# Reordering the first stage of a fused attention and snake-MLP kernel: g product before the rsqrts, one chunk squared on GpSimd, weights loaded later

## Chip, cores, metric

One NeuronCore of a Trainium2 chip, one launch. The metric is the device time in microseconds (us) of one execution, median of several. "Span" is the profiled time from the first to the last instruction, some 2 us less than the device time. A DMA "lands" when all its data has arrived. The "software queue" carries the DMAs that GpSimd issues, the "hardware queue" those of SyncE and ScalarE.

## The reference

```python
q_n, k_n = rmsnorm(q, g_q), rmsnorm(k, g_k)     # q, k, v: 8 batches, 12 heads, 448 tokens, 64
attn = softmax(q_n @ k_n.T / 8)
x = (attn @ v)                                   # as 3584 tokens x 768
h = x @ w_in                                     # 768 x 2048
g = h + sin(alpha * h) ** 2 / (alpha + 1e-9)     # "snake"
out = g @ w_out                                  # 2048 x 768
```

## The kernel before

The kernel runs in stages. In the first, q and k of batch 0 are normalised in three "chunks" of two head pairs, transposed, and made into scores, exponentials and attention values. Then comes the first product of batch 0 (`hps`, 192 matmuls), with the snake step beside it. From there each stage does the attention of the next batch, with the second product of the batch before (`ops`, 896 matmuls in all) cut into fillers between. The program's order is the order on each engine. `S_(n)` is one score tile with n blank matmuls ahead, `A_()` one attention product, `step_of(c, …)` the norm steps of a chunk (0 and 1: squares on GpSimd, 2: the g product folded in, 3 and 4: sums on VectorE, 5: rsqrt and scaling, 6: transposes by DMA and the load of chunk c + 3). NC is 3, so `NC` and `NC + 1` are the fourth and fifth chunk. A "bank" is a piece of PSUM, the memory that TensorE writes; `g_sb` holds the results of the snake step, `osb` the copy of a finished output tile that frees its bank. The first product goes in "pairs" of two snake tiles, counted from 0.

```python
def load_w_in():                              # f32 in memory, bf16 in SBUF, issued by GpSimd
    for hi in range(2):
        nc.gpsimd.dma_start(out=w_in_sb[hi * 64:hi * 64 + 64], in_=rows[hi])
def load_w_out(half):                         # 768 columns in two halves of 384
    nc.gpsimd.dma_start(out=w_out_sb[:, :, cols], in_=src[:, :, cols])
# ... first stage
c0.square(1), c0.square(0)
c0.reduce(1), c0.reduce(0)
c0.rsqrt(slice(1, 2)), c0.rsqrt(slice(0, 1))
keep_busy(BUSY[0], blank)                     # 20 blank matmuls
spread_g()                                    # g_q * g_k to all partitions: matmul, then a ScalarE copy
keep_busy(BUSY[1], blank)                     # 8
c0.fold_g()
# ... v loads, gate on the third chunk
load_w_in()
# ...
S_(), S_(), S_()
c1.rsqrt()
S_(3)
c2.square(0), c2.square(1)                    # on ScalarE
# ...
load_w_out(0)
begin_norm(NC); step_of(NC, 0, 1, 2)()
# ... scores, attention products, fourth and fifth chunk
v_parts[2](), v_parts[3]()
load_w_out(1)                                 # before the first product
A_(), A_()
step_of(NC + 1, 5, 6)()
first_product(0, beside_h(0))
```

"Gate" is a one-column GpSimd copy of a chunk's tile: it holds GpSimd, and so the DMA issues behind it, until that chunk has landed.

Of the kernel before, what the change touches and what calls it, by code (L numbers as in the profile page):

```python
# [32 lines left out]
def kernel(  # L33
# [37 lines left out]
    HALF = D_MODEL // 2  # L71
    BUSY = (20, 8)

# [85 lines left out]

    w_in_sb = wpool.tile([P, KT, D_FF], BF16)  # L160
    w_out_sb = wpool.tile([P, MT, D_MODEL], BF16)
# [19 lines left out]

    def load_w_in():

        rows = moe_w_in.rearrange("(hi pr d) f -> hi d pr f", hi=2, d=D)
        for hi in range(2):
            nc.gpsimd.dma_start(out=w_in_sb[hi * 64:hi * 64 + 64], in_=rows[hi])

# [15 lines left out]
    def norm_tasks(ci):  # L203
# [5 lines left out]
        st.ms = npool.tile([P, 2, 2 * NJ], F32, tag="ms", name="ms")  # L209
        st.inv, st.inv_ps, st.scaled = {}, None, 0  # L210
        st.sq, st.n = {}, None

        def square(w):
            if early:
                rows = g_sb[:, 4 * ci + 2 * w:4 * ci + 2 * w + 2, :].rearrange("p m s -> p (m s)")
                st.sq[w] = rows.bitcast(F32).rearrange("p (a d) -> p a d", d=D)
                nc.scalar.activation(st.sq[w], qk[ci][:, w], ACT.Square)
            else:
                st.sq[w] = npool.tile([P, 2 * NJ, D], F32, tag="sq", name="sq")
                nc.gpsimd.tensor_mul(st.sq[w], qk[ci][:, w], qk[ci][:, w])  # L220
# [7 lines left out]
        def rsqrt(ws=slice(0, 2)):  # L228
            ln = npool.tile([P, 2, 2 * NJ], F32, tag="inv", name="inv")
            if early and st.inv_ps is None:  # L230
                st.inv_ps = bank_pair("inv")
            inv = st.inv_ps[:, :, :2 * NJ] if early else ln
            for w in range(2)[ws]:
                st.inv[w] = inv[:, w, :]
            nc.scalar.activation(ln[:, ws], st.ms[:, ws, :], ACT.Ln, scale=1.0 / D, bias=eps)
            nc.scalar.activation(inv[:, ws], ln[:, ws], ACT.Exp, scale=-0.5)  # L236

        def scale(w):
            eng = nc.vector if early else nc.gpsimd
            if st.n is None:  # L240
                st.n = npool.tile([P, 2, NJ, 2, D], BF16, tag="qkn", name="qkn")
            n, x = st.n[:, w], qk[ci][:, w].rearrange("p (hi j) d -> p hi j d", hi=2)
            inv = st.inv[w].rearrange("p (hi j) -> p hi j", hi=2)
            for hi in range(2):
                eng.tensor_mul(n[:, :, hi, :], x[:, hi], inv[:, hi].unsqueeze(2).to_broadcast([P, NJ, D]))  # L245
            st.scaled += 1
            if early and st.scaled == 2:
                give_back(st.inv_ps, passes() + 3.0)

# [47 lines left out]

    def attend(pi):


        b, hp = pi // NP, pi % NP
        av = bank_pair("av")
        for j in range(NJ):
            for part in range(2):
                for hi in range(2):
                    r = key_rows(pi, hi)
                    o = slice((hi + part) % 2 * 64, (hi + part) % 2 * 64 + 64)
                    nc.tensor.matmul(av[o, part, :S], ones[r, :] if part else vb[b][r, hp, j, :],  # L308
                                     expT[pi // 2, j][r, pi % 2, :], start=(j == 0), stop=(j == NJ - 1))
        rec = rpool.tile([P, S], F32, tag="rec", name="rec")  # L310
        nc.scalar.activation(rec, av[:, 1, :S], ACT.Ln)  # L311
        nc.scalar.activation(rec, rec, ACT.Exp, scale=-1.0)  # L312
        if hp == 0:
            xT[b] = xpool.tile([P, KT, S], BF16, tag="xT", name="xT")
        for hi in range(2):
            r, o = slice(hi * 64, hi * 64 + 64), slice(64 - hi * 64, 128 - hi * 64)
            nc.vector.tensor_mul(xT[b][r, hp, :], av[r, 0, :S], rec[o, :])  # L317
        give_back(av, passes(1.32, 1.06) + 1.4)

# [17 lines left out]
    def first_product(b, beside):  # L337
# [4 lines left out]
        def mm(ps, m, kts):  # L342
            for kt in kts:
                nc.tensor.matmul(ps[:, m % 2, :S], w_in_sb[:, kt, m * P:(m + 1) * P], x[:, kt, :],  # L344
                                 start=(kt == 0), stop=(kt == KT - 1))
# [72 lines left out]
    c0.reduce(1), c0.reduce(0)  # L418
    c0.rsqrt(slice(1, 2)), c0.rsqrt(slice(0, 1))
    keep_busy(BUSY[0], blank)  # L420
    spread_g()
    keep_busy(BUSY[1], blank)
    c0.fold_g()
# [7 lines left out]
    nc.gpsimd.tensor_copy(gate, qk[2][:, 1, 0, 0:1])  # L431
    load_w_in()
    norm[2] = c2 = norm_tasks(2)
    c0.scale(1), c0.scale(0)
    c0.pe_transpose((0, 1), (1,), act=True)
# [11 lines left out]
    def beside_h(b):  # L447

        ci = NC * b + 5
        if ci >= NC * B:  # L450
            return {}
        return {0: [lambda: begin_norm(ci)], 1: [step_of(ci, 0)], 3: [step_of(ci, 1)], 4: [step_of(ci, 3)],
                5: [step_of(ci, 2)], MT // 2: [step_of(ci, 4)]}

    def stage(b):

        tiles = deque((b * NC + c, j) for c in range(NC) for j in range(NJ))
        pairs = deque(b * NP + p for p in range(NP))
        return (lambda warm=0: scores(*tiles.popleft(), warm)), (lambda: attend(pairs.popleft()))

    S_, A_ = stage(0)
    S_(), S_(), S_()
    c1.rsqrt()
    S_(3)
    c2.square(0), c2.square(1)
    c2.fold_g()
    c1.scale(0), c1.scale(1)
    load_qk(NC)
    S_(2), S_(1), S_()
    c1.pe_transpose((0, 1))  # L470
# [5 lines left out]
    load_qk(NC + 2)  # L476
    load_w_out(0)
    begin_norm(NC)
    step_of(NC, 0, 1, 2)()
    A_(), S_(1), S_(1), S_(1)  # L480
    c2.pe_transpose((0, 1))
    v_parts = load_v(1)
    v_parts[0](), v_parts[1]()
    begin_norm(NC + 1)
    step_of(NC + 1, 0, 1, 2)()
    S_(), S_(), S_()
    step_of(NC, 3, 4)()
    A_(), S_(1), A_(), S_(1)
    step_of(NC, 5, 6)()
    S_(1), A_(), S_(1)  # L490
    step_of(NC + 1, 3, 4)()
    S_()
    v_parts[2](), v_parts[3]()
    load_w_out(1)
    A_(), A_()
    step_of(NC + 1, 5, 6)()
    first_product(0, beside_h(0))


# [3 lines left out]
    for b in range(1, B):  # L503
# [9 lines left out]
        if b + 1 < B:  # L513
            at[2] += [lambda: begin_norm(c3), step_of(c3, 0, 1, 2)]
            at[10] += [lambda: begin_norm(c4), step_of(c4, 0, 1)]
            for slot, task in ((9, step_of(c3, 3)), (10, step_of(c3, 4)), (12, step_of(c3, 5)), (12, step_of(c4, 2)),
                               (13, step_of(c4, 3)), (15, step_of(c4, 4)), (17, step_of(c3, 6)), (18, step_of(c4, 5)),
                               (23, step_of(c4, 6))):
                at[slot].append(task)
            for n, part in enumerate(load_v(b + 1)):  # L520
                at[19 + n].append(part)
# [47 lines left out]
```

## Time and profile before

| | before |
|---|---|
| time, us | 441.9 (441.68 to 442.11, 3 runs) |
| span of the profiled run, us | 440.3 |
| TensorE busy | 425.9 us, 97% |
| first product of batch 0 begins | 44.41 |
| second half of w_out issued, landed | 45.62, 70.4 (24.8 us later) |
| second half of w_out needed (49th matmul of the output product) | 74.42 |

The views of this kernel are quoted in the prediction. In the timeline of TensorE stand start, duration, engine, line, operation, count, and in brackets the idle time before it and its releaser.

### The profile page before, as it was taken

What the parts mean: (1) busy time and instruction counts of PE and PEld (TensorE: products, weight loads), DVE (VectorE), ACT (ScalarE), POOL (GpSimd) and SP (SyncE); (2) the same over time, 40 slices, a digit from 0 to 9 for tenths busy, and PEclk for the clock granted to TensorE, in tenths of its full rate; (3) what the DMA queues carried; (4) which work ended last, traced back from release to release, by engine and by line L of the source; (5) the groups of instructions that cost most, each with busy time, mean ns of one, the idle gap of its engine ahead of it and who ended that gap; (6) DMA issues with size and microseconds to landing.
All of it is one profiled execution on the core that took longest, in us unless ns stands there. A gap on an engine that the chain in (4) does not pass through costs nothing.

```text
span 440.3 us, 9454 instructions
## 1 busy us (share of the span) xinstructions
PE 425.9 (97%) x3811; PEld 220.4 (50%) x3811; DVE 228.1 (52%) x331; ACT 340.1 (77%) x531; POOL 278.0 (63%) x262
## 2 busy tenths in 40 slices
PE   7788999899999999999999999999999999999996
PEld 3234544455555554555555555555555555555563
DVE  3576573456544564464645464545645474246611
ACT  4879888878888788887878788887878788788600
POOL 3867978937698287947599196965599285002300
PEclk9679999999999999999999999999999999999999
DMA  7899999592066803596064902598054900420022
GB/s 251 179 237 251 196 220 226 140 227 78 2 197 180 189 2 76 151 221 120 2 198 146 222 2 51 151 207 159 2 162 116 124 0 18 97 56 1 1 71 73
DMA packets 69296, 55.09 MB, mean 125 GB/s; under 512 B 41460, under 2 KB 65796, under 8 KB 69252
## 3 DMA queue, kind: packets, MB, share of 16 engines
q1 hardware_dynamic: 56690, 40.97, 37.2%
q0 software_dynamic: 11616, 11.81, 17.2%
q10 hardware_dynamic: 946, 1.70, 1.0%
q8 instruction: 30, 0.49, 0.5%
q14 instruction: 14, 0.11, 0.1%
HBM read 45.62 MB, written 11.01 MB: 129 GB/s over the span
## 4 chain that ended last, share of the span: by engine, by line
PE 85%; ACT 4%; POOL 3%; issue 2%; DVE 2%; DMA 2%; SPq 0%; POOLq 0%; DVEq 0%
PE hps L344 33%; PE ops L389 32%; PE av L308 12%; PE sc L292 8%; ACT expT L295 3%; POOL sq L220 2%; DMA g_rows<-in_g_q_dram 1%; POOL qk L223 1%; DMA out_dram<-osb 1%; DVE qkn L245 1%; POOL qkn L245 1%; DVE ms L226 0%; ACT rec L311 0%; PE tp L267 0%; DVE g_sb L331 0%
## 5 line engine op out<-in xcount | busy, mean ns | idle before, releaser
L295 ACT ACTIVATE expT<-sc 128x896 bf16<-128x896 f32 x168 | 145.0, 913 | 33.5 <-PE sc L292 32.2
L389 PE MATMUL ops<-w_out_sb,g_sb 128*128 128x384 bf16 x896 | 156.8, 327 | 0.8 <-DVE osb L395 0.7
L344 PE MATMUL hps<-xT,w_in_sb 128*128 128x448 bf16 x768 | 146.7, 353 | 0.0
L326 POOL TENSOR_TENSOR s<-s 128x448 f32<-128x448 f32 x64 | 59.2, 930 | 101.8 <-ACT s L323 91.0
L389 PEld LDWEIGHTS <-g_sb 128*128 128x128 bf16 x896 | 83.1, 98 | 70.9 <-issue 19.5
L331 DVE SCALAR_TENSOR_TENSOR g_sb<-s,inv_alpha_sb,hps 128x448 bf16<-128x448 f32 x128 | 80.7, 678 | 63.1 <-POOL s L326 63.1
L344 PEld LDWEIGHTS <-w_in_sb 128*128 128x128 bf16 x768 | 74.5, 98 | 71.5 <-issue 2.9
L323 ACT ACTIVATE s<-hps,alpha_sb 128x448 f32<-128x448 f32 x128 | 74.5, 627 | 28.0 <-PE hps L344 26.2
L245 POOL TENSOR_TENSOR qkn<-qk,inv 128x448 bf16<-128x448 f32 x84 | 76.1, 937 | 21.8 <-ACT inv L236 21.3
L317 DVE TENSOR_TENSOR xT<-av,rec 64x448 bf16<-64x448 f32 x96 | 59.7, 622 | 52.9 <-ACT rec L312 33.8
L220 POOL TENSOR_TENSOR sq<-qk 128x896 f32<-128x896 f32 x42 | 69.9, 1678 | 6.1 <-DVE ms L226 4.7
L308 PE MATMUL av<-expT,vb 64*64 64x448 bf16 x672 | 70.4, 353 | 1.2 <-ACT expT L295 1.1
L308 PE MATMUL av<-expT,ones 64*64 64x448 bf16 x672 | 70.4, 353 | 0.0
L226 DVE TENSOR_REDUCE ms<-sq 128x14 f32<-128x896 f32 x42 | 45.3, 1083 | 27.5 <-POOL sq L220 27.2
L292 PE MATMUL sc<-qkT 64*64 64x448 bf16 x672 | 52.1, 369 | 2.7 <-DVE qkT L274 1.1
L395 DVE COPY osb<-ops 128x768 f32<-128x768 f32 (+1 forms) x35 | 27.9, 797 | 50.0 <-PE ops L389 44.1
L223 POOL TENSOR_TENSOR qk<-qk,gg 128x896 f32<-128x896 f32 x24 | 50.1, 2088 | 4.9 <-ACT gg L171 3.3
L308 PEld LDWEIGHTS <-vb 64*64 64x64 bf16 x672 | 37.8, 108 | 15.4 <-issue 3.3
L308 PEld LDWEIGHTS <-ones 64*64 64x64 bf16 x672 | 37.3, 108 | 10.8
L328 ACT ACTIVATE s<-s 128x448 f32<-128x448 f32 x64 | 36.9, 577 | 2.9
L292 PEld LDWEIGHTS <-qkT 64*64 64x64 bf16 x672 | 15.1, 106 | 30.6 <-issue 25.8
L311 ACT ACTIVATE rec<-av 128x448 f32<-128x448 f32 x48 | 26.2, 546 | 3.6 <-PE av L308 3.1
(43 smaller groups left out, 138.9 us busy)
## 6 DMA issues: line engine op xcount, KB each, us to landing
qk<-in_q_dram SPq DMA_DIRECT2D x24, 448.0 KB, 4.9
qk<-in_k_dram SPq DMA_DIRECT2D x22, 448.0 KB, 5.4
out_dram<-osb SPq DMA_DIRECT2D x39, 192.0 KB, 2.9
vb<-in_v_dram POOLq DMA_DIRECT2D x32, 168.0 KB, 6.6
w_in_sb<-in_moe_w_in_dram POOLq DMA_DIRECT2D x2, 1536.0 KB, 20.0
w_out_sb<-in_moe_w_out_dram POOLq DMA_DIRECT2D x2, 1536.0 KB, 27.5
out_dram<-osb SPq DMA_DIRECT2D x26, 96.0 KB, 5.8
qk<-in_k_dram ACTq DMA_DIRECT2D x2, 448.0 KB, 6.0
```

Source lines behind the costliest of these rows:

```text
L220: nc.gpsimd.tensor_mul(st.sq[w], qk[ci][:, w], qk[ci][:, w])
L223: eng.tensor_mul(qk[ci][:, 0], qk[ci][:, 0], gg.to_broadcast([P, 2 * NJ, D]))
L245: eng.tensor_mul(n[:, :, hi, :], x[:, hi], inv[:, hi].unsqueeze(2).to_broadcast([P, NJ, D]))
L292: nc.tensor.matmul(sc[key_rows(pp, hi), pp, :S], qkt[r, 1, j * REST:(j + 1) * REST], qkt[r, 0, :], start=True, stop=True)
L295: nc.scalar.activation(expT[c, j], sc[:, :, :S], ACT.Exp, scale=SCALE)
L308: nc.tensor.matmul(av[o, part, :S], ones[r, :] if part else vb[b][r, hp, j, :], expT[pi // 2, j][r, pi % 2, :], start=(j == 0), stop=(j == ...
L317: nc.vector.tensor_mul(xT[b][r, hp, :], av[r, 0, :S], rec[o, :])
L323: nc.scalar.activation(s1, hps, ACT.Sin, scale=alpha_sb[:, m, :])
L326: nc.gpsimd.tensor_mul(s2, s1, s1)
L331: nc.vector.scalar_tensor_tensor(g_sb[:, m, (b % 2) * S:(b % 2 + 1) * S], s2, inv_alpha_sb[:, m, :], hps, op0=ALU.mult, op1=ALU.add)
L344: nc.tensor.matmul(ps[:, m % 2, :S], w_in_sb[:, kt, m * P:(m + 1) * P], x[:, kt, :], start=(kt == 0), stop=(kt == KT - 1))
L389: nc.tensor.matmul(st["ps"][:, k, :HALF], lhsT, w_out_sb[:, m, half * HALF:(half + 1) * HALF], start=(m == 0), stop=(m == MT - 1))
```

## The change

The intent is an earlier first product: the g product no longer stands behind two rsqrts on ScalarE; ScalarE gives two squares to GpSimd; more blank matmuls and a new order of scores keep the TensorE clock up; the fifth chunk, which GpSimd needs, gets the DMA before half of w_in and all of w_out. Core of the diff, cuts marked:

```diff
-    BUSY = (20, 8)
+    BUSY = (11, 15)
-    w_in_sb = wpool.tile([P, KT, D_FF], BF16)
+    w_in_sb = [wpool.tile([P, KT, D_FF // 2], BF16, name=f"w_in_{half}") for half in range(2)]
...                                            # load_w_in(half), matmuls and rsqrt banks accordingly
-            if early:
+            if ci < 2:                         # third chunk: squares on GpSimd
...
-    c0.rsqrt(slice(1, 2)), c0.rsqrt(slice(0, 1))
     keep_busy(BUSY[0], blank)
     spread_g()
+    c0.rsqrt(slice(1, 2)), c0.rsqrt(slice(0, 1))
...
-    load_w_in()
+    load_w_in(0)
+    c2.square(0), c2.square(1)
+    c2.fold_g()
...                                            # scores with 0 0 | 3 | 3 2 2 1 fillers
     load_qk(NC + 2)
-    load_w_out(0)
     begin_norm(NC)
     step_of(NC, 0, 1, 2)()
+    nc.gpsimd.tensor_copy(gate, qk[NC + 1][:, 1, 0, 0:1])
+    load_w_in(1)
+    begin_norm(NC + 1)
+    step_of(NC + 1, 0, 1, 2)()
...
+    load_w_out(0)                              # behind the fourth chunk's scaling
+    v_parts = load_v(1)
+    v_parts[0](), v_parts[1]()
...                                            # the last two attention products side by side: A_(2)
-    v_parts[2](), v_parts[3]()
-    load_w_out(1)
-    A_(), A_()
-    first_product(0, beside_h(0))
+    for i, task in ((2, v_parts[2]), (4, v_parts[3]), (5, lambda: load_w_out(1))):
+        beside.setdefault(i, []).append(task)  # inside the first product
+    first_product(0, beside)
...                                            # later stages: sums of a chunk one slot later
-            ((9, step_of(c3, 3)), (10, step_of(c3, 4)), ..., (13, step_of(c4, 3)), ...
+            ((10, step_of(c3, 3)), (11, step_of(c3, 4)), ..., (14, step_of(c4, 3)), ...
```

More of the change, by code (lines that the diff above doesn't have):

```diff
@@ L180, in spread_alpha, with load_w_in @@
         nc.vector.reciprocal(inv_alpha_sb, alpha_sb)
-    def load_w_in():
+    def load_w_in(half):
         rows = moe_w_in.rearrange("(hi pr d) f -> hi d pr f", hi=2, d=D)
+        cols = slice(half * D_FF // 2, (half + 1) * D_FF // 2)
         for hi in range(2):
-            nc.gpsimd.dma_start(out=w_in_sb[hi * 64:hi * 64 + 64], in_=rows[hi])
+            nc.gpsimd.dma_start(out=w_in_sb[half][hi * 64:hi * 64 + 64], in_=rows[hi, :, :, cols])
     def load_w_out(half):
@@ L209, in norm_tasks @@
         st.ms = npool.tile([P, 2, 2 * NJ], F32, tag="ms", name="ms")
-        st.inv, st.inv_ps, st.scaled = {}, None, 0
+        st.inv, st.inv_ps, st.scaled = {}, [], 0
         st.sq, st.n = {}, None
         def square(w):
-            if early:
+            if ci < 2:
                 rows = g_sb[:, 4 * ci + 2 * w:4 * ci + 2 * w + 2, :].rearrange("p m s -> p (m s)")
@@ L229, in rsqrt @@
             ln = npool.tile([P, 2, 2 * NJ], F32, tag="inv", name="inv")
-            if early and st.inv_ps is None:
-                st.inv_ps = bank_pair("inv")
-            inv = st.inv_ps[:, :, :2 * NJ] if early else ln
+            inv = bank_pair("inv") if early else ln
+            if early:
+                st.inv_ps.append((inv, passes(0.0, 0.55) + 2.4))
             for w in range(2)[ws]:
-                st.inv[w] = inv[:, w, :]
+                st.inv[w] = inv[:, w, :2 * NJ]
             nc.scalar.activation(ln[:, ws], st.ms[:, ws, :], ACT.Ln, scale=1.0 / D, bias=eps)
-            nc.scalar.activation(inv[:, ws], ln[:, ws], ACT.Exp, scale=-0.5)
+            nc.scalar.activation(inv[:, ws, :2 * NJ], ln[:, ws], ACT.Exp, scale=-0.5)
         def scale(w):
@@ L246, in scale @@
             st.scaled += 1
-            if early and st.scaled == 2:
-                give_back(st.inv_ps, passes() + 3.0)
+            if st.scaled == 2:
+                for ps, time in st.inv_ps:
+                    give_back(ps, time)
         def transpose():
@@ L296, in scores, with attend @@
         give_back(sc, passes(0.2 + 0.2 * warm, 0.82) + 0.2)
-    def attend(pi):
+    avs = {}
+    def attend(pi, tiles=range(NJ)):
         b, hp = pi // NP, pi % NP
-        av = bank_pair("av")
-        for j in range(NJ):
+        if tiles[0] == 0:
+            avs[pi] = bank_pair("av")
+        av = avs[pi]
+        for j in tiles:
             for part in range(2):
@@ L309, in attend @@
                                      expT[pi // 2, j][r, pi % 2, :], start=(j == 0), stop=(j == NJ - 1))
+        passes(0.19 * len(tiles))
+        if tiles[-1] < NJ - 1:
+            return
         rec = rpool.tile([P, S], F32, tag="rec", name="rec")
@@ L317, in attend @@
             nc.vector.tensor_mul(xT[b][r, hp, :], av[r, 0, :S], rec[o, :])
-        give_back(av, passes(1.32, 1.06) + 1.4)
+        give_back(avs.pop(pi), passes(0.0, 1.06) + 1.4)
     def snake(b, ps, m):
@@ L343, in mm @@
             for kt in kts:
-                nc.tensor.matmul(ps[:, m % 2, :S], w_in_sb[:, kt, m * P:(m + 1) * P], x[:, kt, :],
+                nc.tensor.matmul(ps[:, m % 2, :S], w_in_sb[m * 2 // MT][:, kt, m % (MT // 2) * P:(m % (MT // 2) + 1) * P], x[:, kt, :],
                                  start=(kt == 0), stop=(kt == KT - 1))
@@ L452, in beside_h @@
         return {0: [lambda: begin_norm(ci)], 1: [step_of(ci, 0)], 3: [step_of(ci, 1)], 4: [step_of(ci, 3)],
-                5: [step_of(ci, 2)], MT // 2: [step_of(ci, 4)]}
+                MT // 2: [step_of(ci, 2, 4)]}
     def stage(b):
@@ L458, in stage, with values @@
         pairs = deque(b * NP + p for p in range(NP))
-        return (lambda warm=0: scores(*tiles.popleft(), warm)), (lambda: attend(pairs.popleft()))
+        def values(n=1):
+            if n == 1:
+                return attend(pairs.popleft())
+            for js in (range(NJ - 1), [NJ - 1]):
+                for pi in list(pairs)[:n]:
+                    attend(pi, js)
+        return (lambda warm=0: scores(*tiles.popleft(), warm)), values
     S_, A_ = stage(0)
-    S_(), S_(), S_()
+    S_(), S_()
     c1.rsqrt()
     S_(3)
-    c2.square(0), c2.square(1)
-    c2.fold_g()
     c1.scale(0), c1.scale(1)
     load_qk(NC)
-    S_(2), S_(1), S_()
+    S_(3), S_(2), S_(2), S_(1)
     c1.pe_transpose((0, 1))
@@ L476 @@
     load_qk(NC + 2)
-    load_w_out(0)
     begin_norm(NC)
     step_of(NC, 0, 1, 2)()
+    nc.gpsimd.tensor_copy(gate, qk[NC + 1][:, 1, 0, 0:1])
+    load_w_in(1)
+    begin_norm(NC + 1)
+    step_of(NC + 1, 0, 1, 2)()
     A_(), S_(1), S_(1), S_(1)
     c2.pe_transpose((0, 1))
+    S_(2), A_(), S_(2)
+    step_of(NC, 3, 4)()
+    S_(2), S_(1), A_()
+    step_of(NC, 5, 6)()
+    load_w_out(0)
     v_parts = load_v(1)
     v_parts[0](), v_parts[1]()
-    begin_norm(NC + 1)
-    step_of(NC + 1, 0, 1, 2)()
-    S_(), S_(), S_()
-    step_of(NC, 3, 4)()
-    A_(), S_(1), A_(), S_(1)
-    step_of(NC, 5, 6)()
-    S_(1), A_(), S_(1)
+    S_(1), S_(1), A_(), S_()
     step_of(NC + 1, 3, 4)()
-    S_()
-    v_parts[2](), v_parts[3]()
-    load_w_out(1)
-    A_(), A_()
+    S_(), A_(2)
     step_of(NC + 1, 5, 6)()
-    first_product(0, beside_h(0))
+    beside = beside_h(0)
+    for i, task in ((2, v_parts[2]), (4, v_parts[3]), (5, lambda: load_w_out(1))):
+        beside.setdefault(i, []).append(task)
+    first_product(0, beside)
     PLAN = "6 SS 7 SS 7 SSS 8 SSS 8 SSAS 7 SS 5 SSASA 4 S 4 SSAAA"
@@ L515 @@
             at[10] += [lambda: begin_norm(c4), step_of(c4, 0, 1)]
-            for slot, task in ((9, step_of(c3, 3)), (10, step_of(c3, 4)), (12, step_of(c3, 5)), (12, step_of(c4, 2)),
-                               (13, step_of(c4, 3)), (15, step_of(c4, 4)), (17, step_of(c3, 6)), (18, step_of(c4, 5)),
+            for slot, task in ((10, step_of(c3, 3)), (11, step_of(c3, 4)), (12, step_of(c3, 5)), (12, step_of(c4, 2)),
+                               (14, step_of(c4, 3)), (15, step_of(c4, 4)), (17, step_of(c3, 6)), (18, step_of(c4, 5)),
                                (23, step_of(c4, 6))):
```

## The prediction

> **What bounds the kernel now.** I read the page's slices first, then the engines' busy time in long windows, then who waited on TensorE, then the timelines of ScalarE, GpSimd and VectorE in the first 60 us, and last the DMA issues by window.
>
> The slices: TensorE's busy tenths, and the clock granted to it.
>
> ```profile
> PE   7788999899999999999999999999999999999996
> ...
> PEclk9679999999999999999999999999999999999999
> ```
>
> One slice is 11 us. Only the first four have a TensorE that is not full, and only the first three a reduced clock. The page's mean clock of 0.984 fits about 13.7 us at half speed, from 14.9 to 28.6 us. The busy time of the engines in long windows (window, length, then busy time of PE, PEld, DVE, ACT, POOL, then clock, DMA share, GB/s):
>
> ```profile
> 45.00:95.00 50.00, 47.99 (x444) 25.01 (x443) 26.53 (x41) 41.71 (x68) 41.95 (x40) 1.00 1.06 203
> 95.00:145.00 50.00, 50.00 (x460) 26.12 (x458) 26.91 (x38) 41.58 (x65) 36.54 (x33) 1.00 0.49 121
> ```
>
> From 95 us TensorE is full to the last stage: its list of waits after 45 us has two entries, both in the second batch's stage.
>
> ```profile
> PE sc L292 <- DVE osb L395: 1.0, 1, 1.0
> PE ops L389 <- DVE osb L395: 0.7, 1, 0.7
> ```
>
> So nothing can be won after about 95 us; the time is "when the first product of batch 0 begins", plus TensorE work that the change leaves alone, plus new waits. That begin is 44.41 us here. Before it TensorE is not the bound. The timeline of the start (start, duration, engine, line, count, and in brackets idle time before and its releaser):
>
> ```profile
> 9.33 0.21 ACT L171 COPY gg<-gps 128x64 f32<-128x64 f32 x1
> 9.42 1.15 DVE L245 TENSOR_TENSOR qkn<-qk,inv 128x448 bf16<-128x448 f32 x2 [0.59 <-ACT inv L236]
> 9.61 2.08 POOL L223 TENSOR_TENSOR qk<-qk,gg 128x896 f32<-128x896 f32 x1 [3.29 <-ACT gg L171]
> 11.72 1.15 DVE L245 TENSOR_TENSOR qkn<-qk,inv 128x448 bf16<-128x448 f32 x2 [1.15 <-POOL qk L223]
> 14.60 2.54 ACT L295 ACTIVATE expT<-sc 128x896 bf16<-128x896 f32 x3 [1.64 <-PE sc L292]
> 18.39 1.78 ACT L217 ACTIVATE g_sb<-qk 128x896 f32<-128x896 f32 x2
> 24.34 0.92 ACT L295 ACTIVATE expT<-sc 128x896 bf16<-128x896 f32 x1 [1.74 <-PE sc L292]
> 28.80 0.54 ACT L311 ACTIVATE rec<-av 128x448 f32<-128x448 f32 x1 [0.99 <-PE av L308]
> ```
>
> The first exponential (14.60) stands at the end of a chain: copy of g to all rows, fold on GpSimd, scaling on VectorE, transposes, scores. From there to the end of the 21st exponential (42.72) ScalarE is the bound: 21 exponentials at a pitch of 0.83 (17.4), two squares (1.7), three rsqrt pairs at 0.55 (1.65), four reciprocals at 1.06 (4.25): 25.0 of 28.1 us, and the 3.1 left are its waits (1.74, 0.99, 0.15, 0.18). Then 1.7 us of the last two attention products run before the first product.
>
> **What the Trainium skill says.** "TensorE: Matmul & The Clock Gate", Part 1: the array runs at half clock until one window of about 3.4 us is busy, and goes back after an idle one, with windows that run freely. The trace agrees: half clock lasts 13.65 us, four such windows, and starts after a window (11.5 to 14.9) that has some 1 us of ordinary matmuls. Part 4 of the same page says that transposes don't count as busy for this gate; the trace fits (the transposes of 21.0 to 22.5 did not wake it), without proving it. "DMA: Bandwidth & Descriptors", Queues, rings and completion order: each DMA engine takes queues in turn, packet by packet. The trace agrees: the fifth chunk, issued at 20.0 beside the w_in load, reached GpSimd only at 37.08, though chunks in a freer stretch land in 5 to 7 us. "PSUM — Partial Sum Buffer", Specifications (TRN2): GpSimd cannot read PSUM, so it is fed by ScalarE in the snake step, which is what the trace shows.
>
> **The change part by part.**
>
> 1. *g copied ahead of the rsqrts.* The copy moves from 9.33 to behind the two squares, 7.56. The fold starts at 7.85 and ends at 9.93 (2.08) instead of 11.69. The two rsqrts get separate PSUM tiles, so the key scaling no longer waits for both (the 0.59): it runs 8.85 to 10.0, and the query scaling 10.0 to 11.2 instead of 12.87. Transposes 0.48, copies 0.69 and scores as before put the first exponential at 12.9: 1.7 us won.
> 2. *Third chunk squared on GpSimd.* Takes 2 x 0.85 = 1.7 us from ScalarE and puts 2 x 1.67 on GpSimd at 16.3, before the fold of that chunk (ends 21.7). The reduce that needs it stands behind the second chunk's copies (19.8), so this is off the path.
> 3. *Order and clock.* The warm-up matmuls last to about 10.1 instead of 9.5, scores begin at 12.3, and with 3, 3, 2, 2, 1 fillers ahead of the scores the window 11.5 to 14.9 holds some 2.4 us of matmuls. I expect the clock to stay up. Second-chunk transposes then take 0.84 instead of 1.44 and come at 17.8 instead of 21.0.
> 4. *Last two pairs together.* After the last exponential only two seventh tiles (0.4 us) remain in place of 1.7; but the sixth product's bank is one that the 20th exponential frees, so 0.4 of it is lost again.
>
> Walking ScalarE down its new order: exp 1-2 from 12.9; rsqrt waits for VectorE's reduces until 14.85 (idle 0.3); exp 3-7 end 19.55; exp 8 waits for the second chunk's copies until 20.2 (0.65); exp 8-10 and rsqrt end 23.25; first reciprocal 24.3; exp 11-13 end 26.8; exp 14 waits for the bank of the first attention product (1.0); exp 14 to 28.7; reciprocal 29.8; exp 15-17 to 32.3; reciprocal and rsqrt to 33.9; exp 18-19, reciprocal, exp 20-21 end at 38.3. Two last tiles and latency: the first product begins at about 39.1 instead of 44.4, **5.3 us earlier**.
>
> What comes back:
>
> 5. *GpSimd.* Its squares of the fifth chunk wait for VectorE's reduce of the fourth (32.2); then squares 3.3, fold 2.1, scaling 3.6, two weight and two v issues 2.5, scaling 3.6, first snake square 0.9: 48.2. VectorE's first two snake sums end at 49.5, begin + 10.4. TensorE needs that bank back at begin + 4 x 2.28 = 9.1. Before, these were 52.6 - 44.4 = 8.2. So **1.3 us** are lost.
> 6. *Weights.* w_in's first half lands near 30 (needed 39), the second, issued at about 28 behind the fifth chunk, near 44 (needed 48): hidden. w_out's first half moves from 21.4 to 41, lands near 56, needed at 58.7: just hidden. The second half is issued behind the sixth even snake square, about 57.5 instead of 45.6. It took these landings before:
>
> ```profile
> w_out_sb<-in_moe_w_out_dram POOLq DMA_DIRECT2D x1, 1536.0 KB, 24.8
> w_out_sb<-in_moe_w_out_dram POOLq DMA_DIRECT2D x1, 1536.0 KB, 30.3
> ```
>
> Most of those 25 to 30 us were queueing behind other software loads; the software queue moved its bytes in some 12 us (DMA view, in short windows). It would land at 69 to 72; it is needed about 11 us after the first product's end, at 70. Expected loss **1 us**, between 0 and 4.
> 7. *Second stage.* The third osb copy now stands ahead of the reduce that held it up; of the 1.7 us of waits I take **0.7** as won. Moving the reduce and fold tasks in later stages cannot win anything on a full TensorE.
>
> Sum: -5.3 + 1.3 + 1.0 - 0.7 = -3.7: 438.2. The order looks tuned against just these waits, so I shade it a little: **437.8 us**.
>
> **Rivals.** A: *everything hidden.* The path falls by 5.3 and the stage waits of 1.7 vanish, no loss: 435. For it: GpSimd and DMA estimates have slack of 1 to 3 us. Against: GpSimd's queue of 16 us between chunk five's squares and the first snake square is made of measured durations. B: *the gain becomes a wait for weights or GpSimd.* With loads 16 to 20 us later on a DMA that is at a share of 1.06 from 45 to 95, TensorE stands still before the second product or inside the first: up to 4 us more, 441. For it: the saturated DMA; against: w_in's first half needs only half the bytes early, so total work is not more. C: *the clock still falls.* If the window 21.8 to 25.2 (about 1.5 us of matmuls in my walk) counts as idle, half clock comes a little later; the attention products take 2.6 instead of 1.3 and 1 to 2 us go: 439.
>
> **Range and chances.** A and B span 435 to 441; 434.8 to 441.2 is the range. Over 2% faster needs under 433.1, 8.8 us won: even ScalarE without any wait could begin the first product only at about 37, 7.4 us earlier, plus all of 1.7; that is 4 in 100. Slower by 2% needs 450.7, which only a long weight stall would do: 2 in 100. Within 2%: 94.
>
> **What would show it.** Right: the copy of gg near 7.6, first exponential near 12.9, no squares of 896 elements on ScalarE after 13 us, the clock row full in slices two and three, first product near 39, the fifth chunk landed before 28. Step 5 shows as idle time on TensorE near begin + 9 with VectorE or ScalarE behind it; step 6 as idle time ahead of the second product's first or 49th matmul. The prediction is wrong if the begin does not move by 4 us or more, or if it moves and TensorE then idles over 4 us before 95 us.

## More of the kernel before

```profile
74.42 2.11 PE L389 MATMUL ops<-w_out_sb,g_sb 128*128 128x384 bf16 x12 [0.71 <-DVE osb L395]
...
81.60 0.57 PE L292 MATMUL sc<-qkT 64*64 64x448 bf16 x8 [0.99 <-DVE osb L395]
```

The first matmuls that read the second half of w_out wait 0.71 us for a VectorE copy that frees a bank, not for the weights, which had been there for 4 us.

## The result

The changed kernel took 453.46 us (453.01 to 454.55, 4 runs), beside 442.0 for the kernel before (441.68 to 442.69). The ratio is 1.0261, 95% interval 1.0239 to 1.0283: slower. A ratio here is the mean time of one kernel's fast runs over that of the other's of the same rounds, so not quite the ratio of the medians quoted. In some experiments the profiled run stands outside the rounds and is not in the ratio; it is said where that matters (e5).

The page of the changed kernel, TensorE's busy tenths and its granted clock, in slices of 11.3 us:

```profile
PE   8889992699999999999999999999999999999996
...
PEclk9999997789999999999999999999999999999999
```

The first slices are what the change was for: fuller, and at full clock. The seventh and eighth (68 to 90 us) hold a hole that was not there, and the clock falls in it and behind it. The start, in the timelines of ScalarE and of GpSimd:

```profile
7.46 0.19 ACT L171 COPY gg<-gps 128x64 f32<-128x64 f32 x1
...
12.73 1.73 ACT L297 ACTIVATE expT<-sc 128x896 bf16<-128x896 f32 x2 [0.33 <-PE sc L294]
```

```profile
7.73 2.09 POOL L224 TENSOR_TENSOR qk<-qk,gg 128x896 f32<-128x896 f32 x1 [1.42 <-ACT gg L171]
...
41.51 1.22 POOL L192 DMA_DIRECT2D w_out_sb<-in_moe_w_out_dram  x1
...
57.53 1.21 POOL L192 DMA_DIRECT2D w_out_sb<-in_moe_w_out_dram  x1
```

The g copy stands at 7.46 instead of 9.33, the first exponential at 12.73 instead of 14.60. The two halves of w_out are issued at 41.51 and 57.53. TensorE's timeline from there:

```profile
39.57 9.26 PE L353 MATMUL hps<-xT,w_in 128*128 128x448 bf16 x48
49.86 9.24 PE L353 MATMUL hps<-xT,w_in 128*128 128x448 bf16 x48 [1.03 <-DVE g_sb L340]
...
81.53 3.54 PE L398 MATMUL ops<-w_out_sb,g_sb 128*128 128x384 bf16 x12 [10.35 <-DMA w_out_sb<-in_moe_w_out_dram]
...
91.25 0.96 PE L294 MATMUL sc<-qkT 64*64 64x448 bf16 x8 [2.11 <-DVE osb L404]
92.14 3.03 PE L398 MATMUL ops<-w_out_sb,g_sb 128*128 128x384 bf16 x10
```

The first product begins 4.84 us earlier (39.57 against 44.41) and ends 3.40 earlier (59.18 against 62.58). Then TensorE stands still for 10.35 us ahead of the first matmul that reads the second half of w_out. The 12 matmuls behind it take 3.54 us where they took 2.11, at half clock, and ten later ones 3.03 instead of 1.80. The list of what TensorE waited for (us in total, times, longest):

```profile
PE ops L398 <- DMA w_out_sb<-in_moe_w_out_dram: 10.3, 1, 10.3
PE sc L294 <- DVE osb L404: 2.1, 1, 2.1
...
PE hps L353 <- DVE g_sb L340: 1.0, 1, 1.0
```

And the chain of what released what, followed back from the end, between 55 and 95 us (start, duration, what):

```profile
57.53 23.96 DMA w_out_sb<-in_moe_w_out_dram
...
81.53 3.54 PE ops L398 x12
```

For 24 us the end of the kernel hangs on one transfer. The account by differences of the two spans (451.6 - 440.3 = 11.3):

| point | before | after | difference |
|---|---|---|---|
| first product begins | 44.41 | 39.57 | -4.84 |
| first product ends | 62.58 | 59.18 | -3.40 |
| second half of the output product begins | 74.42 | 81.53 | +7.11 |
| end of the span | 440.3 | 451.6 | +11.3 |

The last 4.2 us, between 81.53 and the end, are 1.43 and 1.23 of slow matmuls (3.54 - 2.11, 3.03 - 1.80), 1.12 more of the wait for `osb` (2.11 - 0.99) and some 0.4 elsewhere.

### The profile page after: what moved, and what is told of

The parts are those of the page before. It is cut to its first block, busy times and chain, and to the rows that moved or that the text cites. A ratio compares the mean times of both kernels' runs of the same rounds, so it can differ in the third digit from the quotient of the medians.

```text
span 451.6 us, 9465 instructions
## 1 busy us (share of the span) xinstructions
PE 427.5 (95%) x3819; PEld 220.9 (49%) x3819; DVE 227.6 (50%) x331; ACT 338.3 (75%) x529; POOL 283.2 (63%) x267
## 4 chain that ended last, share of the span: by engine, by line
PE 81%; DMA 6%; POOL 6%; ACT 3%; DVE 2%; issue 1%; DVEq 0%; POOLq 0%; ACTq 0%
PE ops L398 32%; PE hps L353 28%; PE av L314 12%; PE sc L294 8%; DMA w_out_sb<-in_moe_w_out_dram 5%; POOL qkn L246 2%; ACT expT L297 1%; DMA qk<-in_k_dram 1%; POOL qk L224 1%; POOL vb L135 1%; POOL sq L221 1%; POOL s L335 1%; DVE g_sb L340 1%; PE sc L290 0%; DVE xT L326 0%
## 5 line engine op out<-in xcount | busy, mean ns | idle before, releaser
L398 PE MATMUL ops<-w_out_sb,g_sb 128*128 128x384 bf16 x896 | 159.5, 330 | 10.6 <-DMA w_out_sb<-in_moe_w_out_dram 10.3
L353 PE MATMUL hps<-xT,w_in 128*128 128x448 bf16 x768 | 146.8, 353 | 1.0 <-DVE g_sb L340 1.0
L398 PEld LDWEIGHTS <-g_sb 128*128 128x128 bf16 x896 | 83.8, 99 | 83.1 <-issue 21.5
L353 PEld LDWEIGHTS <-w_in 128*128 128x128 bf16 x768 | 74.5, 98 | 72.7 <-issue 4.2
L332 ACT ACTIVATE s<-hps,alpha_sb 128x448 f32<-128x448 f32 x128 | 74.6, 627 | 28.3 <-PE hps L353 23.9
L221 POOL TENSOR_TENSOR sq<-qk 128x896 f32<-128x896 f32 x44 | 73.4, 1683 | 1.1 <-DVE ms L227 0.7
L314 PE MATMUL av<-expT,vb 64*64 64x448 bf16 x672 | 69.2, 349 | 1.1 <-ACT expT L297 0.9
L314 PE MATMUL av<-expT,ones 64*64 64x448 bf16 x672 | 69.2, 349 | 0.0
L227 DVE TENSOR_REDUCE ms<-sq 128x14 f32<-128x896 f32 x44 | 46.8, 1081 | 16.3 <-POOL sq L221 16.1
L321 ACT ACTIVATE rec<-rec 128x448 f32<-128x448 f32 x48 | 27.7, 577 | 1.5
## 6 DMA issues: line engine op xcount, KB each, us to landing
w_in<-in_moe_w_in_dram POOLq DMA_DIRECT2D x4, 768.0 KB, 11.3
```

The lines of the kernel that those rows point to most:

```text
L221: nc.gpsimd.tensor_mul(st.sq[w], qk[ci][:, w], qk[ci][:, w])
L314: nc.tensor.matmul(av[o, part, :S], ones[r, :] if part else vb[b][r, hp, j, :], expT[pi // 2, j][r, pi % 2, :], start=(j == 0), stop=(j == ...
L332: nc.scalar.activation(s1, hps, ACT.Sin, scale=alpha_sb[:, m, :])
L353: nc.tensor.matmul(ps[:, m % 2, :S], w_in_sb[m * 2 // MT][:, kt, m % (MT // 2) * P:(m % (MT // 2) + 1) * P], x[:, kt, :], start=(kt == 0), ...
L398: nc.tensor.matmul(st["ps"][:, k, :HALF], lhsT, w_out_sb[:, m, half * HALF:(half + 1) * HALF], start=(m == 0), stop=(m == MT - 1))
```

## The experiments

The theory after this reading (theory 1): the second half of w_out lands too late because it is issued 12 us later into DMA queues that are as full as before. Rivals: the loss is mostly the clock; it is lateness as such; it is only what stands ahead of it in the software queue (GpSimd's own DMAs); or only what flows beside it. "Landing" and "waits" in what follows are those of the one profiled run of each kernel; the times are of all runs. The table, for orientation, gives the second half of w_out in each kernel that moved it or its neighbours:

| kernel | issued | us to land | landed | TensorE waits for it |
|---|---|---|---|---|
| before | 45.6 | 24.8 | 70.4 | 0 |
| after | 57.5 | 24.0 | 81.5 | 10.35 |
| e1, right behind the first half | 42.8 | 28.2 | 71.0 | 0 |
| e2, before, but issued late | 62.1 | 12.5 | 74.6 | 0 |
| e4, at the second pair | 51.1 | 23.4 | 74.5 | 2.83 |
| e5, nothing of w_out ahead of it | 57.4 | 22.8 | 80.2 | 10.0 |
| e9, no chunk loads beside it | 57.2 | 20.9 | 78.1 | 7.16 |
| e13, both | 56.5 | 15.9 | 72.4 | 3.02 |

**e1: the second half issued right behind the first.**

```diff
     load_w_out(0)
+    load_w_out(1)
-    for i, task in ((2, v_parts[2]), (4, v_parts[3]), (5, lambda: load_w_out(1))):
+    for i, task in ((2, v_parts[2]), (4, v_parts[3])):
```

> The changed kernel with the second half of w_out issued directly behind the first half (about 42.7 us instead of 57.5), ahead of the v loads. Theory 1 (the load is issued too late; it needs some 24 us from issue to landing as in both kernels): it lands near 67 to 70, when the 49th output matmul wants it, the 10.3 us wait goes, the clock stays up, and the time is 437 to 440, below the kernel before. Theory 2 (the DMA has to carry the same bytes before that point and is full, so an earlier issue only queues longer): it still lands near 80 and the time stays over 448.

442.83 us (441.9 to 444.09), ratio 1.0023 (1.0003 to 1.0043). The DMA wait is gone, and with it all of the loss against before. The gain does not show, as three smaller waits take it: the stall in the first product is 2.15 us, because the second issue puts 1.2 us more on GpSimd ahead of its first snake square; the `osb` wait is 2.24; and the clock dips from 52.6 to 56.0.

**e2: the kernel before, with only the second half issued late.**

```diff
-    load_w_out(1)
     A_(), A_()
...
-    first_product(0, beside_h(0))
+    beside = beside_h(0)
+    beside.setdefault(5, []).append(lambda: load_w_out(1))
+    first_product(0, beside)
```

> The kernel before with this one thing of the change: the second half of w_out issued at the sixth snake pair of batch 0 (about 60 us instead of 45.6). Theory 1: landing near 84 against a need at 74.4, a wait of about 10 us ahead of the 49th output matmul and then some 3 to 4 us at half clock and in bunched waits: 453 to 457. Theory 3 (the loss comes from the new order of the start as a whole, which crowds the second stage): under 445.

442.76 us (442.6 to 443.11), ratio 1.0012: no loss. The expectation failed. Issued later than in the changed kernel, the same transfer landed in 12.5 us, at 74.6, 0.8 us before TensorE wanted it; what TensorE waits for is still the bank:

```profile
75.41 2.11 PE L389 MATMUL ops<-w_out_sb,g_sb 128*128 128x384 bf16 x12 [0.71 <-DVE osb L395]
```

The DMA queues in the window 68 to 70 us (packets, MB, share of 16 engines; only the software queue has a line):

```profile
q0 software_dynamic: 533, 0.41, 131.6%
```

The software queue has the DMA to itself there and moves 0.41 MB in 2 us. So lateness as such costs nothing; what else is in the DMA at that time decides.

**e3: the clock held up through the wait.** 46 blank matmuls ahead of the 49th output matmul, into the same bank.

```diff
+    if b == 0 and halves == (1,) and i == 0:
+        for _ in range(46):
+            nc.tensor.matmul(st["ps"][:, 0], blank[:, :P], blank, start=True, stop=True)
```

> The changed kernel with 46 blank matmuls (9.9 us at full clock) ahead of the 49th output matmul, so that TensorE is busy while it would wait for w_out; the landing is not touched. If the half clock after the wait costs time by itself, 12 and 10 output matmuls fall from 3.5 and 3.0 us to 2.1 and 1.8 and the time is 450 to 451.5. If the clock costs nothing (other waits hide it), it stays at 453.5.

451.11 us (450.27 to 451.7), ratio 1.0199, against 1.0261: 2.3 us less. The matmuls behind the wait run at full speed again (2.11 us for 12, where the changed kernel took 3.54):

```profile
81.18 2.11 PE L401 MATMUL ops<-w_out_sb,g_sb 128*128 128x384 bf16 x12
```

The blanks don't shorten the wait: the matmuls start at 81.18, against 81.53. They even hid part of an improvement, as the transfer landed after 22.1 us in this run, at 79.6, and the blanks ran on past it. A second spell of half clock, behind the `osb` wait, stays (ten matmuls in 3.30 us). So the clock is some 2 us of the loss (2.3 by the medians; 1.43 of it shows in the first 12 matmuls), and a consequence of the wait; the rival "mostly the clock" falls.

**e4: the second half at the second pair of the first product,** ahead of the last two v parts.

```diff
-    for i, task in ((2, v_parts[2]), (4, v_parts[3]), (5, lambda: load_w_out(1))):
+    for i, task in ((1, lambda: load_w_out(1)), (2, v_parts[2]), (4, v_parts[3])):
```

> The changed kernel with the second half of w_out issued at the second snake pair instead of the sixth (about 50 instead of 57.5 us), ahead of the third and fourth part of v. Theory 1 (issue time decides, landing follows it): lands near 73 to 75, wait of 3 to 5 us, time 443 to 447. Theory 2 (full DMA decides): lands near 79 to 80, time over 451.

445.1 us (444.73 to 447.64), ratio 1.0077. Issued 6.4 us earlier, it lands 7.0 earlier, and the wait shrinks by 7.5 (10.35 to 2.83). In e1, issued 14.7 us earlier, it landed 10.5 earlier. So an earlier issue brings an earlier landing here, though not always by the same amount.

**e5: the first half earlier, the second left late.** The first half is issued directly behind w_in's second half, at 32.4 instead of 41.5.

```diff
     load_w_in(1)
+    load_w_out(0)
...
-    load_w_out(0)
```

> The changed kernel with only the FIRST half of w_out moved: it is issued directly behind the second half of w_in (about 32 us instead of 41.5), into the stretch in which the software queue moved little. The second half stays where the change put it (about 57). Theory 4 (backlog: at 57.5 the queue still held the rest of the first half and four v parts, and the second half began only behind them): the queue is clear by 57, the second half lands in 12 to 17 us as in the run where only it was late, at 70 to 74; the wait falls from 10.3 to 1 to 4 us and the time is 441 to 445. Theory 1 alone (late issue, 24 us to land whatever stands before it): landing at 81, wait 10, time 452 to 454.

449.39 us (448.12 to 452.8), ratio 1.0148. The first half landed at 53.6, before the second was issued, yet in the profiled run the second still took 22.8 us:

```profile
80.29 4.02 PE L398 MATMUL ops<-w_out_sb,g_sb 128*128 128x384 bf16 x12 [10.00 <-DMA w_out_sb<-in_moe_w_out_dram]
```

That run is the slowest of the four (452.8; the others took 448.12 to 450.09, and the ratio is of these three), so the others probably waited less, and their landing was not traced. "Only what stands ahead of it" had named 441 to 445 us; all four runs are above that, so as the whole cause it is refuted. That it counts for little is not shown: by the ratios the edit is worth 5.0 us (1.0261 against 1.0148).

**e6: both halves earlier, GpSimd's chain not longer.** First half behind w_in's second half, second half where the changed kernel has the first.

```diff
     load_w_in(1)
+    load_w_out(0)
...
-    load_w_out(0)
+    load_w_out(1)
...                                            # and no load_w_out(1) in the first product
```

> The changed kernel with the first half of w_out behind the second half of w_in (32 us) and the second half in the first half's old place (about 42). Both theories of the wait: it is gone. GpSimd's chain ahead of the first snake square is some 0.5 us longer, so the wait inside the first product is 1 to 2 us; the wait of 2.1 us on an output copy in the second stage stays. Time 438 to 441.

441.02 us (440.63 to 441.86), ratio 0.9971 (0.9955 to 0.9987). The matmuls that read the second half wait for nothing:

```profile
70.85 2.12 PE L398 MATMUL ops<-w_out_sb,g_sb 128*128 128x384 bf16 x12
```

The stall in the first product is 1.24, the `osb` wait 2.23, and behind it the clock is at half from about 80.4 to 83.8 us.

**e7: GpSimd's chain shortened,** by issuing the second half and all v parts inside the first product (pairs 0 to 4).

```diff
-    load_w_out(1)                              # of e6
-    v_parts[0](), v_parts[1]()
-    for i, task in ((2, v_parts[2]), (4, v_parts[3])):
+    for i, task in ((0, lambda: load_w_out(1)), (1, v_parts[0]), (2, v_parts[1]), (3, v_parts[2]), (4, v_parts[3])):
```

> As the run before, but with the second half of w_out and the four v parts issued behind the first snake squares (pairs 0 to 4) instead of ahead of them: 1.3 and 1.2 us of issuing leave GpSimd's chain ahead of the first square. My account of step 5 (that chain sets when the bank of the first product comes free): the wait inside the first product (1.0 us in the changed kernel) is gone, time 436.5 to 439. If the chain was not the reason, 1 us of wait stays and the time is that of the run before.

442.1 us (440.31 to 443.37), ratio 0.999 (0.9959 to 1.002), so not told apart from e6, and the time expected was missed. The stall in the first product goes, but 1.3 us of waiting for `g_sb` come back at the start of the output product: it seems that GpSimd's issues have only moved to hold up other snake squares. The profiled run also had two spells of half clock (26.9 to 30.3 and 81.5 to 85), and the runs of this one kernel lie 3 us apart.

**e8: e7, with a sum moved behind the bank's copy.** In batch 1 only, the two sums of the last chunk one slot (one place in the stage's order) later on VectorE.

```diff
-    (14, step_of(c4, 3)), (15, step_of(c4, 4)), ...
+    (14 + (b == 1), step_of(c4, 3)), (15 + (b == 1), step_of(c4, 4)), ...
```

> As the run before, and in the second batch's stage alone the two sums of the eighth chunk's squares stand behind the fourth output copy on VectorE instead of one ahead of it. The wait of TensorE on that copy, 2.1 us in the changed kernel and 1.0 in the one before, falls by the 1.1 us of one sum: time 435.5 to 438. If the copy waits for the two multiplications ahead of it alone, nothing changes.

439.05 us (438.9 to 439.08), ratio 0.9923 (0.9908 to 0.9938). The wait for `osb` is back from 2.2 to about what it was before the change, and the clock stays up in the profiled run (mean 1.0, where e7's was 0.99). The wait is 1.1 of the 3 us gained on e7; the rest may be the clock, which this pair of runs does not separate:

```profile
78.40 0.57 PE L294 MATMUL sc<-qkT 64*64 64x448 bf16 x8 [1.11 <-DVE osb L404]
```

**e9: the loads beside it taken away.** The changed kernel, with the loads of the eighth and ninth chunk put off to 74 us.

```diff
-    step_of(NC + 1, 5, 6)()
+    step_of(NC + 1, 5)()
+    norm[NC + 1].transpose()                   # step 6 without its load
...
-    at[7].append(step_of(c2, 6))
+    at[7].append(norm[c2].transpose if b == 1 else step_of(c2, 6))
...
-    at[10] += [lambda: begin_norm(c4), step_of(c4, 0, 1)]
+    at[10] += [lambda: [load_qk(7), load_qk(8)] if b == 1 else None, lambda: begin_norm(c4), step_of(c4, 0, 1)]
```

> The changed kernel with w_out untouched (second half issued at 57.5), but the loads of the eighth and ninth chunk, which run beside it from 61 us on, put behind the first six stores of the second stage (about 71 us or later). Theory 5 (contention: beside a chunk load the software queue moves 0.18 MB in 2 us, alone 0.40, so the hardware queue's chunk loads and transposes stretch the landing): the second half lands at 73 to 77 instead of 81.5 and TensorE's wait for it falls from 10.3 to 2 to 6 us, though the chunks then come later and other waits may grow. Theory 4 (backlog in the software queue alone): landing at 80 to 82, wait 9 to 11.

451.52 us (450.85 to 452.43), ratio 1.0202. The transfer takes 20.9 us instead of 24.0, and TensorE waits 7.16:

```profile
78.16 4.02 PE L398 MATMUL ops<-w_out_sb,g_sb 128*128 128x384 bf16 x12 [7.16 <-DMA w_out_sb<-in_moe_w_out_dram]
```

So "only the chunk loads beside it" is refuted: they are some 3 us. It is a weak test of all that flows beside it. From issue to landing the hardware queue still sent 3989 packets (1.55 MB), against 4374 (2.40 MB) in the changed kernel: the transposes and stores stayed, and the put-off loads began at 74.

**e10: a best version.** e6, with e8's move, and the snake squares of tiles 0 and 2 of batch 0 on ScalarE, so that the first product never waits for GpSimd.

```diff
-        if m % 2 == 0:
+        if m % 2 == 0 and (b or m > 2):        # else squared on ScalarE
```

> Both halves of w_out early as in e6_wout_both_early, the sums behind the output copy in the second stage as in e8, and the squares of the first and third snake tile of batch 0 on ScalarE instead of GpSimd, so that VectorE's first snake sum does not stand at the end of GpSimd's chain. If that chain is what delays the bank (step 5), the wait inside the first product (1.0 to 1.2) is gone without coming back as the 1.3 us wait on g_sb that e8 had: 436.5 to 438.5, clock 1.0 throughout. If not, as e8: 439.

439.0 us (438.67 to 439.52), ratio 0.9922. The first product runs its 18.3 us without a stall:

```profile
41.13 18.33 PE L353 MATMUL hps<-xT,w_in 128*128 128x448 bf16 x96
```

Yet it is no faster than e8 (0.9923), and the 436.5 to 438.5 expected were missed. In its profiled run the clock was 0.50 from 27 to 30 us and the first product began at 41.13, against 39.45 in e8, where the clock was 1.00 there. That cannot be all, as another run of e10 had a mean clock of 1.0 and took 439.12.

**e11: e10 with the rsqrts ahead of the g copy again,** the first part of the change undone alone.

```diff
+    c0.rsqrt(slice(1, 2)), c0.rsqrt(slice(0, 1))
     keep_busy(BUSY[0], blank)
     spread_g()
-    c0.rsqrt(slice(1, 2)), c0.rsqrt(slice(0, 1))
```

> The run before with step 1 of the prediction undone alone: the two rsqrts stand ahead of the copy of g again. Step 1 is worth the 1.7 us by which the first exponential then moves from 12.7 to 14.4: 1.5 to 2 us slower than the run before. If ScalarE had slack behind it, under 0.5.

440.99 us (440.81 to 441.81), ratio 0.9966 against 0.9922 for e10 on the same chip: that part is worth 2.0 us (predicted 1.7).

**e12: e10 with w_in's second half behind its first,** without the gate: the deferral of w_in undone alone.

```diff
     load_w_in(0)
+    load_w_in(1)
...
-    nc.gpsimd.tensor_copy(gate, qk[NC + 1][:, 1, 0, 0:1])
-    load_w_in(1)
```

> The run e10_best with both halves of w_in issued one after the other behind the third chunk, so that the fifth chunk's load shares the DMA with all of it, as before the change. Deferring the second half is worth the time by which the fifth chunk lands earlier (30.5 against 37 in the kernel before): GpSimd's squares of that chunk then start at about 37 instead of 33 and its chain ends 4 us later; with the first squares on ScalarE part of it is hidden: 1 to 4 us slower than e10_best. If the chain has slack, the same time.

437.9 us (437.29 to 438.98), ratio 0.9895 (0.9876 to 0.9914): the fastest version, by the medians 1.1 us better than e10. The intervals just overlap, and e10's profiled run had a spell of half clock at the start that e12's did not have, so this is not shown to be a gain. The expectation failed: beside e10's other edits, nothing is lost without the deferral. The fifth chunk had landed in time; GpSimd's squares of it waited for VectorE, as its timeline says:

```profile
32.53 3.31 POOL L221 TENSOR_TENSOR sq<-qk 128x896 f32<-128x896 f32 x2 [3.54 <-DVE ms L227]
```

Two more runs were made for the two points still open: whether backlog and chunk loads explain the landing together, and why the deferral of w_in was not needed.

**e13: the edits of e5 and e9 together.**

> The changed kernel with two things at once that each did little alone: w_out's first half issued right behind w_in's second half (nothing of it left in the software queue by 57 us), and the loads of the eighth and ninth chunk put off to 74 us. w_out's second half stays where the change has it (issued near 57.4). Theory 1a (its landing time is the sum of what is queued ahead and what flows beside it): with both away it lands in 12 to 17 us, by 70 to 75, and TensorE waits 0 to 4 us ahead of the 49th matmul of the output product; 443 to 446 us. Rival 1b (the DMA transposes, which stay, are what holds the software queue back): it still takes 18 to 21 us and lands at 76 to 78.5, with a wait of 6 to 8.5 us and 448 to 452 us.

444.95 us (443.29 to 447.36), ratio 1.0053 (1.0016 to 1.0091). The transfer landed after 15.9 us, and TensorE waited 3.02 us:

```profile
72.40 3.46 PE L398 MATMUL ops<-w_out_sb,g_sb 128*128 128x384 bf16 x12 [3.02 <-DMA w_out_sb<-in_moe_w_out_dram]
```

This is inside what theory 1a named (12 to 17 us, 0 to 4 of wait). By the profiled runs the two are worth 1.2 and 3.1 us of the landing when removed alone, and 8.1 together. That they don't add is not shown, as e5's profiled run was its slowest: by the ratios e5 is worth 5.0 us of time (4.0 with the profiled run counted in), e9 2.6 and e13 9.2, not far from the sum. What the queues do show is the sharing. The changed kernel in the window 66 to 68 us, then e13 in the window 62 to 64:

```profile
q0 software_dynamic: 323, 0.25, 88.9%
q1 hardware_dynamic: 316, 0.08, 44.7%
```

```profile
q0 software_dynamic: 513, 0.40, 128.7%
q1 hardware_dynamic: 32, 0.00, 1.6%
```

In the changed kernel both queues have work, and in most windows of 2 us they send the same number of packets (323 and 316; in 70 to 72 us, beside a chunk load, 224 and 225, with 0.17 MB for the software queue), though not in all (243 and 607 in 62 to 64). In e13 the hardware queue had by then sent most of what it had, and the software queue moves 0.40 MB in 2 us, as much as alone in e2.

One thing stays open. In e5 and in e13, from 54 to 62 us, the software queue sent hardly anything (0.01 to 0.09 MB per 2 us), though a v part was pending, and w_out from about 57. In e2 the software queue began to flow some 2 us after the issue, in e13 only some 5. What holds it back there these runs do not tell. A lead: in seven of these eight windows of 2 us the hardware queue's packets alone took 98 to 148% of the 16 engines, with only 0.08 to 0.70 MB, and a DMA transpose was issued in that stretch. Rival 1b of e13 (the transposes hold the software queue back) is refuted for the landing as a whole, which came at 72.4 and not at 76 to 78.5, but not for this stretch.

**e14: e12 with w_in in one tile,** two DMAs with whole rows instead of four with half rows.

```diff
-    w_in_sb = [wpool.tile([P, KT, D_FF // 2], BF16, name=f"w_in_{half}") for half in range(2)]
+    w_in_sb = wpool.tile([P, KT, D_FF], BF16)
-    load_w_in(0)
-    load_w_in(1)
+    load_w_in()
```

> The fastest kernel so far (e12, 437.9 us) with w_in as one tile again, moved in two DMAs with whole rows instead of four with half rows. If the size of the packets decides how the fifth chunk shares the DMA with w_in, the fifth chunk comes later: GpSimd's squares of it, which stood at 32.5 us behind a sum of VectorE, wait for the DMA and start after 34 us, and TensorE stalls 1 to 4 us more inside the first product: 439 to 442 us. If packet size is nothing, the squares start within 0.5 us of 32.5 and the time is 437.3 to 438.7; then the whole rearrangement of w_in is worth nothing.

439.39 us (438.66 to 440.0), ratio 0.9921 (0.9905 to 0.9938). The two kernels ran on different chips, so their ratios are compared: 0.9921 - 0.9895 is 0.0026, or 1.1 us, with intervals that just overlap. The mechanism shows in GpSimd's timeline, where the second square of the fifth chunk now waits for the load:

```profile
35.19 1.68 POOL L220 TENSOR_TENSOR sq<-qk 128x896 f32<-128x896 f32 x1 [0.96 <-DMA qk<-in_k_dram]
```

The k half of the chunks loaded in that stretch took a median of 17.1 us to land instead of 12.5. So with w_in in half rows the chunk lands earlier; this is what the split is good for. TensorE did not pay inside the first product as I had expected, but ahead of the second stage's scores, where it waits 1.8 us for transposes instead of 1.1, and 0.3 for `g_sb`.

## Why the prediction was wrong

By its own steps:

1. *g copied early*: right. First exponential at 12.73 (predicted 12.9); the part by itself is worth 2.0 us (e11), predicted 1.7.
2. *Third chunk's squares on GpSimd*: right; they run at 15.96 and nothing waits for them.
3. *Clock*: right for the start in this run, but not safely: e7 and e10 have the same order of the start, and in their profiled runs the clock was 0.50 from 27 to 30 us and the first product began at 41.17 and 41.13. That is rival C, and some 1.6 us. The clock that falls later is behind the long wait and was not foreseen.
4. *Walk to the first product*: right. 39.57, predicted 39.1; 4.84 us won, predicted 5.3.
5. *GpSimd's chain*: right. First snake square done at 48.5, predicted 48.2; stall 1.03, predicted 1.3.
6. *Weights*: w_in was hidden as predicted. The first half of w_out was hidden by a hair: it landed at 59.1, not 56, and was needed at 59.18. The second half was issued at 57.53, predicted 57.5. **The failed step is its last term: "It would land at 69 to 72 … Expected loss 1 us, between 0 and 4." It landed at 81.5, and the loss was 10.35 us.**
7. *Second stage*: half wrong. The wait of 0.7 vanished (e6, where no wait for the DMA covers it), but the later one grew from 0.99 to 2.11, as the sum moved out of the way of one copy stands ahead of the next. e8 moved it again and got it back to 1.11.

In the failed step I split the old 24.8 us into 12 of the transfer's own flow and the rest of queueing ahead, and let the rest vanish. The 12 is good for a transfer alone: e2 measured 12.5. But the queueing did not vanish, and it was not only ahead. From issue to landing the software queue moved 2.23 MB in the changed kernel, of which 1.57 were this transfer, so 0.66 MB stood ahead of it. At the rate of a software queue alone (0.41 MB per 2 us, e2) 2.23 MB take 10.9 us. With the slow start that e2 had, an estimate is 12.5 us for the transfer and 3.2 for the 0.66 MB ahead, 15.7 in all. It took 24.0. In that time the hardware queue sent 2.40 MB in 4374 packets, the software queue 2864. By these estimates the sharing is 8 to 13 us, more than the 3.2 of the queue ahead; the two were not separated cleanly by an experiment, as e9 left most hardware packets in place. I had named the turn by packet for the fifth chunk and did not apply it to the weights. Before, the same crowded stretch did no harm, since the transfer was issued 12 us earlier and needed 3.2 us later (74.42 against 81.53 - 10.35 = 71.18).

Rival B had the mechanism, a gain that turns into a wait for weights, and the size wrong: "up to 4 us more". The rest of the miss is some 2 us of clock behind the wait (e3) and the longer `osb` wait of step 7. Without its term for the weights the prediction's sum gives 437.2; e6, where the weights come in time, took 441.0. Its `osb` wait was 2.23 instead of the 1.0 left in the sum, and ten matmuls behind it took 2.82 us instead of 1.80, so step 7 was a second, smaller error. Where the load is issued early (e6, e10, e12), the time falls below the kernel before. That e12 ends at 437.9, near the number predicted, is no credit to the prediction: it has other edits too.

## What to carry to other kernels

A load moved later must be priced by what the DMA queues carry in its new window, not by its old time minus the queue that stood ahead of it: read packets and MB of each queue there. In this case the software queue sent 533 packets in 2 us alone, and 224 to 323 where the hardware queue had work too. When a change speeds up the start, go through every load with a deadline behind it, since the deadlines come earlier by the same amount. And a load deferred to make room for another should be checked alone: here no gain of the deferral of w_in was found (e12), while that of w_out cost the whole gain.

## What the Trainium skill lacked or had wrong

- "DMA: Bandwidth & Descriptors", Anatomy of one DMA: its fit of 2.0 us plus bytes over 436 GB/s gives, as an estimate, 9.2 us for the 3.1 MB of f32 that the second half of w_out reads. The runs show 12.5 us with little beside it (e2) and 15.9 to 28.2 beside other traffic. The section could say that the fit is for an idle DMA.
- Same page, Queues, rings and completion order: the turn by packet agrees with the traces in most windows (323 packets against 316 in the same 2 us). What follows is not said there: packet size sets the share. 323 packets of the software queue were 0.25 MB, 316 of the hardware queue 0.08; and with w_in in half rows the k halves of the chunks beside it landed in 12.5 us instead of 17.1 (e12, e14), which fits, though no run counts their turns.
- "TensorE: Matmul & The Clock Gate", Part 1: it puts the return to half clock behind an idle window of about 3.4 us. Half clock after the 10.35 us wait, at a cost of some 2 us (e3), agrees. But stalls of 2.15 us (e1) and 2.23 (e6) were each followed by some 3.3 us at a clock of 0.50 as well, in e1 with about 1.25 us of matmuls in the 3.4 us before, and another of 2.24 (e1) was not. So a much shorter stall can already cost the clock, and need not.
- Same page, same part: it puts the ramp penalty under 1% of a typical kernel span. The runs of e7 went from 440.31 us (mean clock 0.999) to 443.37 (0.99): 0.7%, within that, but as much as most effects measured.
